# Whole 128x128 transposes in a window-attention kernel, in place of blocks cut to 64 or 96 query rows

## The chip, the cores and the metric

The kernel runs on one core of a Trainium2 chip. The metric is the time of one execution on the device, in microseconds (us), the median of several runs. The core has engines that run side by side, each through its own list of instructions in order, tied together by semaphores: TensorE (PE: matrix products and transposes, with the loads of its stationary operand shown apart as PEld), VectorE (DVE), ScalarE (ACT), GpSimd (POOL), and SyncE (SP), which issues the transfers.

## The reference, cut to what matters

Windowed attention with some global tokens, then a feed-forward network. 8 batches, 8 heads, 512 local and 32 global positions, 64 numbers a head; the network is 512 to 2048 to 512, on 4352 rows.

```python
k_all, v_all = cat([k_g, k_l]), cat([v_g, v_l])
out_g = softmax(q_g @ k_all.T / 8) @ v_all                 # 32 global queries see all 544 keys
s_ll = where(abs(i - j) <= 32, q_l @ k_l.T / 8, -1e9)      # a local query sees its window ...
s_l = cat([q_l @ k_g.T / 8, s_ll])                         # ... and the 32 global keys
out_l = softmax(s_l) @ v_all
x = heads side by side                                     # [8 * 544, 512]
h = relu(x @ w_in)
out = (s * h * h + b) @ w_out
```

The result is float32. The kernel keeps most products near that by splitting an operand into a rounded part and a rest and adding the partial products.

## The kernel before, in words

Work goes by slots: one slot is one head of one half (256 queries) of one batch, 8 x 2 x 8 = 128 slots. A half has two blocks of 128 queries. The scores of a block are a tile with the 128 queries on the partitions and 192 or 224 keys in the columns; both blocks' columns lie side by side in `sm`, 416 columns (line 30). After the softmax (lines 192 to 217) the weights must have the keys on the partitions for the product with the values, so they are transposed on PE, in two chunks of 128 key columns for a block (table `CHUNKS`, line 32). The first chunk's keys reach only a part of the block's queries, 64 or 96 of them; the second has the global keys and is wanted for all 128. A slot so has four transposes (`p_transposes`, line 287): one of 64 query rows, one of 96 and two of 128. In the first half the 64 rows are queries 64 to 127, in the second 0 to 63. They fill 64 + 128 + 96 + 128 = 416 columns of one PSUM tile `ps_t`.

From slot 16 on (`NF`), ACT copies `ps_t` to SBUF as the rounded part (`p_split`, line 361), DVE makes the rest (line 362), and the products with the values (`pv_products`, line 372) follow in the next slot, woven in between the next head's transposes by `transposes_and_pv` (line 391). Slots 0 to 15 use plain float32 products (`transposes32`, `pv32`) while the network's weights are being brought from float64 words into split float32 by DVE, ACT and POOL (`weight_piece`, line 105; 32 pieces).

The feed-forward runs behind, 12 slots later (`LAG`): each step is 24 products of 256 columns (`ffn_in`, line 494), an activation of ACT and DVE (lines 500 to 511), and 12 products of 512 columns (`ffn_out`, line 526). The global queries' weights are transposed as whole blocks (`g_transposes`, line 424), four and then one for a group of heads.

The order on each engine is set by a list scheduler when the program is built; it goes by its own estimates, and the source order is only its start. A change of one kind of instruction so moves others.

Of the kernel before, what the change touches and what calls it, by code (L numbers as in the profile page):

```python
# [18 lines left out]
B, H, SL, SG, D = 8, 8, 512, 32, 64  # L19
DM, DF = 512, 2048  # L20
P = 128
HALF = 256
KW = 224
NEG = -8.0e9
# A block's columns: [32 keys before | own 128 | 32 global | 32 keys after]; the sequence's first block has
# [32 global | own 128 | 32 keys after], its last [32 keys before | own 128 | 32 global].
# Per (half, block): the columns within the half's 416, and the two chunks of 128 of them that are  # L27
# transposed and meet the values: (first column, first query, queries). The first chunk's keys reach
# a part of the queries only, the second has the global keys.
NC = 416  # L30
COLS = {(0, 0): slice(0, 192), (0, 1): slice(192, NC), (1, 0): slice(0, 224), (1, 1): slice(224, NC)}
CHUNKS = {
# [6 lines left out]
BIG = 3.0e38  # L39


# The first batch's heads run with plain float32 products while the weights are being prepared.
NF = 16
AHEAD = 0
LAG = 12
# Where a piece of the weights is prepared: buffers that have no other use yet.
SPOTS = (["a","b","c","c","xs"]+["c","c","a","b"]*1+["a","b","c","c"]*12)[:32]
PIECES = [2, 2, 2, 2, 2, 2, 2, 2, 2, 2, 3, 3, 3, 3]
NORM_POOL = lambda j: j < NF
# [11 lines left out]
def f32(ap):  # L61
    return ap.bitcast(F32)
# [3 lines left out]
def window_attention_then_ffn(ctx: ExitStack, tc: tile.TileContext, qd, qg, kw, vw, vg, w_in, w_out, sv, bv, out):  # L66
    nc = tc.nc
# [8 lines left out]
    ident = const.tile([P, P], F32, name="ident")  # L76
# [1 line left out]
    s_t = const.tile([P, 1], F32, name="s_t")  # L78
    b_t = const.tile([P, 1], F32, name="b_t")

    # additive masks over a block's columns
    masks = {}
    for first, parts in ((True, ((32, 192, 0),)), (False, ((0, 160, 0), (192, 224, 32)))):
        mask = const.tile([P, 192 if first else 224], BF16, name=f"mask{int(first)}")
        nc.gpsimd.memset(mask, 0.0)
        # the window's key c - skip against query p: p <= c - skip <= p + 64
        for c0, c1, skip in parts:
            for sign, base in ((1, c0 - skip), (-1, 64 - c0 + skip)):
                nc.gpsimd.affine_select(
                    out=mask[:, c0:c1], in_=mask[:, c0:c1], pattern=[[sign, c1 - c0]], compare_op=ALU.is_ge,  # L90
                    fill=NEG, base=base, channel_multiplier=-sign,
                )
        masks[first] = mask
# [3 lines left out]

    xg_d = dram.tile([B * SG, DM], F32, name="xg_d")

    # The weights come as float64: a piece's words are put together as float32, with the exponent  # L100
    # bounded to float32's range (smaller is 0, larger not finite) and the mantissa rounded.
    exp_b = const.tile([P, 1], F32, name="exp_b")
    nc.vector.memset(exp_b, -896.0 * 2.0**23)

    def weight_piece(k):
        c = k // 2
        spot = SPOTS[k]
        queue = nc.scalar if k < ACT_DMA else nc.sync
        if spot == "xs":
            both = sb.tile([P, 2048], I32, tag="xs", name=f"wst{k}", bufs=1)  # L110
            st, e = both[:, 0:1024], both[:, 1024:1536]
        else:
            tags = {"a": ("kq", 1024, 3, "vsg", 1280, 1), "b": ("pg", 1280, 1, "qgs", 512, 1), "g": ("g", 1024, 2, "r", 512, 2),
                    "c": ("kq", 1024, 3, "vs", 512, 2)}
            t1, n1, b1, t2, n2, b2 = tags[spot]
            st = sb.tile([P, n1], I32, tag=t1, name=f"wst{k}", bufs=b1)[:, 0:1024]
            e = sb.tile([P, n2], I32, tag=t2, name=f"we{k}", bufs=b2)[:, 0:512]
        if k % 2 == 0:
            queue.dma_start(st, w_in[c])
            hi, lo = wi[:, 0, :, c * P:(c + 1) * P], wi[:, 1, :, c * P:(c + 1) * P]  # L120
            shape = lambda ap: ap.rearrange("p (c f) -> p c f", c=4)
        else:
            queue.dma_start(st, w_out[c * P:(c + 1) * P, :])
            hi, lo = wo[:, 0, c, :], wo[:, 1, c, :]
            shape = lambda ap: ap
        words = st.rearrange("p (n w) -> p n w", w=2)
        low, high = words[:, :, 0], words[:, :, 1]
        # 2^e with the sign
        nc.vector.tensor_scalar(  # L129
            out=e, in0=high, scalar1=20, scalar2=0x7FF, op0=ALU.logical_shift_right, op1=ALU.bitwise_and,  # L130
        )
        nc.scalar.activation(out=e, in_=e, func=AF.Relu, bias=exp_b, scale=2.0**23)
        nc.scalar.activation(out=low.bitcast(F32), in_=low.bitcast(U32), func=AF.Copy, scale=2.0**-52)
        nc.vector.scalar_tensor_tensor(  # L134
            out=e, in0=high, scalar=-(1 << 31), in1=e, op0=ALU.bitwise_and, op1=ALU.bitwise_or,
        )
        # 1 + the mantissa: 8 + 20 bits of the high word, less 7, and the low word
        nc.vector.tensor_scalar(  # L138
            out=high, in0=high, scalar1=0xFFFFF, scalar2=0x41000000, op0=ALU.bitwise_and, op1=ALU.bitwise_or,
        )  # L140
        m = high.bitcast(F32)
        nc.vector.scalar_tensor_tensor(out=m, in0=m, scalar=7.0, in1=low.bitcast(F32), op0=ALU.subtract, op1=ALU.add)  # L142
        w = f32(e)
        nc.gpsimd.tensor_tensor(out=w, in0=m, in1=w, op=ALU.mult)
        nc.scalar.copy(out=hi, in_=shape(w))
        (nc.gpsimd if k in POOL_LO else nc.vector).tensor_sub(out=lo, in0=shape(w), in1=f32(hi))

# [1 line left out]
    NS = B * 2 * H  # L149
    st_ = {}  # L150

    def slot(j):
        return j // 16, (j // 8) % 2, j % 8
# [62 lines left out]
            )  # L216
        st_["p", j] = sm

    # a half's keys for the global queries: the global ones and 0 to 223, or 224 to 511
    def own(k, hf):  # L220
        n, c = (192, P) if hf == 0 else (240, 144)
        return k[:, 0:2 * n].rearrange("p (k c) -> p k c", k=2)[:, :, 0:c]

    def sg_rows(j):
        b, hf, h = slot(j)
        if hf == 0 and h % 4 == 0:
            st_["sg", b, h // 4] = sb.tile([P, SGW], F32, tag=f"sg{h // 4}", name=f"sg{j}", bufs=1)
        r0 = 32 * (h % 4)
        return st_["sg", b, h // 4][r0:r0 + 32]
# [47 lines left out]
    def chunks(j):  # L277
        b, hf, h = slot(j)
        o = 0
        for blk in range(2):  # L280
            for c in range(2):
                c0, q0, n = CHUNKS[hf, blk][c]
                yield blk, c, c0, q0, n, slice(o, o + n)
                o += n

    # yields after each block's transposes
    def p_transposes(j):
        sm = st_.pop(("p", j))
        p_t = ps.tile([P, 512], F32, tag="t", name=f"ps_t{j}")
        st_["pst", j] = p_t[:, 0:NC]  # L290
        for blk, c, c0, q0, n, o in chunks(j):
            q = slice(q0, q0 + n)
            nc.tensor.transpose(out=p_t[:, o], in_=sm[q, c0:c0 + P], identity=ident[q, q])  # L293
            if c == 1:
                yield

# [41 lines left out]
    def scores(j):  # L338
        b, hf, h = slot(j)
        ks, qs = st_.pop(("ks", j)), st_.pop(("qs", j))  # L340
        p_s = ps.tile([P, 512], F32, tag="s", name=f"ps_s{j}")
        for blk in range(2):
            cols = COLS[hf, blk]
            for a in range(2):
                nc.tensor.matmul(  # L345
                    p_s[:, cols], lhsT=qs[:, a, blk * P:(blk + 1) * P], rhs=ks[:, cols], start=(a == 0), stop=(a == 1),
                )
        p_g = ps.tile([P, 512], F32, tag="g", name=f"ps_g{j}")
        qgh = st_["qgs", b][:, h]
        ng = 256 + 32 * hf  # L350
        nc.tensor.matmul(p_g[0:64, 0:ng], lhsT=qgh, rhs=own(ks, hf), start=True, stop=True)  # L351
        softmax(j, p_s)
        # rows of the global queries: qh.k + ql.k
        tg = sb.tile([P, 288], F32, tag="tg", name=f"tg{j}", bufs=1)
        nc.scalar.copy(out=tg[0:32, 0:ng], in_=p_g[32:64, 0:ng])
        nc.vector.tensor_add(out=sg_rows(j)[:, hf * 256:hf * 256 + ng], in0=p_g[0:32, 0:ng], in1=tg[0:32, 0:ng])
# [7 lines left out]

    xcur = {}

    # yields after each block's products
    def pv_products(j):
        pt, vs = st_.pop(("pt", j)), st_.pop(("vs", j))
        p_o = st_["pso", j] = ps.tile([P, 2, 2, P], F32, tag="o", name=f"ps_o{j}")  # L370
# [16 lines left out]
            out=x[q0:q0 + 64, h // 2, :].rearrange("p (k q) -> p k q", k=2), in0=u[0:64], in1=u[64:128],  # L387
        )

    # The last products of a block are shorter than the load of the next values' chunk: transposes go between.  # L390
    def transposes_and_pv(jt, jp):
        t = p_transposes(jt) if NF <= jt < NS else iter(())
        p = pv_products(jp) if NF <= jp < NS else iter(())
# [6 lines left out]
        if NF <= jt < NS:  # L400
            p_split(jt)

# [1 line left out]
    def g_softmax(b, g):  # L404
        v = st_["sg", b, g]
        gm = sb.tile([P, 1], F32, tag="gm", name=f"gm{b}_{g}")
# [20 lines left out]
            nc.scalar.copy(out=ph, in_=v)  # L427
            nc.vector.tensor_sub(out=pl, in0=v, in1=f32(ph))

    # by pairs of heads  # L430
    def g_load(b, h):
        rv = sb.tile([P, 10 * D], F32, tag="rvg", name=f"rvg{b}_{h}", bufs=1)
        nc.sync.dma_start(rv, vg[b, h // 2])
# [20 lines left out]
        nc.vector.tensor_add(out=xr.rearrange("q (h d) -> q h d", h=2), in0=t[:, :, 0], in1=t[:, :, 1])  # L454
        nc.sync.dma_start(xg_d[b * SG:(b + 1) * SG, h * D:(h + 2) * D], xr)

# [1 line left out]
    NT = 17  # L458
    xs_ = {}

# [114 lines left out]
    piece = 0  # L575
# [3 lines left out]
    for j in range(NM + LAG + 2):  # L579
# [3 lines left out]
        for _ in range(PIECES[j] if j < len(PIECES) else 0):  # L583
            weight_piece(piece)
            piece += 1
# [106 lines left out]
```

## Time and profile before

| what | value |
|---|---|
| median of 3 runs | 1111.67 us (1111.55 to 1111.82) |
| profiled execution, first to last instruction | 1109.8 us |
| PE busy | 1064.7 us, 96% |
| DVE busy | 872.3 us, 79% |
| ACT busy | 722.4 us, 65% |
| POOL busy | 426.9 us, 38% |
| granted TensorE clock, mean share of full speed | 0.984 |

The median is 1.9 us over the profiled span; the profile gives no other time for its own execution than this span. A matmul's end in the trace is modelled and matmuls overlap, so a row's busy time is not what the matmul costs; the distance from one start to the next, or the length of a piece in the chain of waits, is.

### The profile page before, as it was taken

Reading aid. Unit: us, or ns where it says so; the run is one execution under the profiler, and the core shown is the slowest. Engines: PE = TensorE matmul, PEld = TensorE weight load, DVE = VectorE, ACT = ScalarE, POOL = GpSimd, SP = SyncE. Lnnn points to the kernel's source line nnn. Section 1 sums busy time; section 2 is a strip of 40 time slices with the busy share of each in tenths; the row PEclk is TensorE's granted clock in tenths of the full one; section 3 lists DMA queues with packets and bytes.
Section 4 is the critical chain, followed back from the end, with each engine's and each line's share of the span. In section 5 each row is a group of like instructions: output and inputs, shape, how many; then the busy total and the mean of one; then the engine's idle time right before and its main releaser. Section 6 shows DMA issues by size and latency. Waiting matters only on the chain.

```text
span 1109.8 us, 20489 instructions
## 1 busy us (share of the span) xinstructions
PE 1064.7 (96%) x7048; PEld 930.7 (84%) x7048; DVE 872.3 (79%) x2119; ACT 722.4 (65%) x1828; POOL 426.9 (38%) x457
## 2 busy tenths in 40 slices
PE   4889879999999999999999999999999999999996
PEld 2457668889989889898998999989989899998885
DVE  7999998789778977798778977897789777964221
ACT  6666767677667766686767775776678676844221
POOL 6887774343224423343323433442344242411000
PEclk9968999999999999999999999999999999999998
DMA  6454422232213212231223221321223121201000
GB/s 231 149 164 140 153 67 87 69 95 72 63 50 93 77 37 93 66 91 54 82 62 95 67 69 46 106 72 44 78 65 100 45 93 56 85 6 45 20 20 19
DMA packets 63536, 86.80 MB, mean 78 GB/s; under 512 B 7624, under 2 KB 50632, under 8 KB 63432
## 3 DMA queue, kind: packets, MB, share of 16 engines
q1 hardware_dynamic: 63144, 84.44, 24.9%
q8 instruction: 56, 0.92, 0.3%
q10 hardware_dynamic: 288, 1.05, 0.2%
q14 instruction: 48, 0.39, 0.1%
HBM read 76.02 MB, written 9.44 MB: 77 GB/s over the span
## 4 chain that ended last, share of the span: by engine, by line
PE 84%; DVE 12%; issue 1%; DMA 1%; ACT 0%; POOL 0%; DVEq 0%
PE acc L526 33%; PE ps_h L494 32%; PE ps_t L293 7%; PE ps_s L345 4%; PE ps_o L372 4%; DVE we L134 2%; DVE wst L138 2%; DVE we L129 2%; PE ps_og L446 2%; DVE wst L142 2%; PE ps_g L351 1%; DVE g L509 1%; DVE ss L210 1%; DVE sm L201 1%; PE ps_tg L424 1%
## 5 line engine op out<-in xcount | busy, mean ns | idle before, releaser
L494 PE MATMUL ps_h<-xs,wi 128*128 128x256 f32 x3264 | 445.4, 283 | 3.1 <-DVE r L501 2.0
L526 PE MATMUL acc<-wo,g 128*128 128x512 f32 x1632 | 431.1, 399 | 4.9 <-DVE g L509 2.7
L494 PEld LDWEIGHTS ps_h<-xs,wi 128*128 128x128 f32 x3264 | 420.2, 190 | 18.2 <-DVE r L501 2.5
L526 PEld LDWEIGHTS acc<-wo,g 128*128 128x128 f32 x1632 | 289.9, 189 | 59.5 <-DVE g L509 3.6
L189 POOL TENSOR_TENSOR vs<-rv,vs 128x256 fp32r<-128x256 f32 x112 | 94.9, 847 | 221.4 <-ACT vs L188 215.6
L501 DVE SCALAR_TENSOR_TENSOR r<-ps_h,s_t,r 128x512 f32<-128x512 f32 x136 | 101.5, 746 | 70.6 <-ACT r L500 70.1
L508 ACT ACTIVATE g<-r,b_t 128x512 fp32r<-128x512 f32 x136 | 98.2, 722 | 63.4 <-DVE r L501 62.5
L509 DVE SCALAR_TENSOR_TENSOR g<-r,b_t,g 128x512 fp32r<-128x512 f32 x136 | 109.3, 803 | 38.2 <-ACT g L508 36.5
L500 ACT ACTIVATE r<-ps_h 128x512 f32<-128x512 f32 x136 | 81.1, 597 | 85.8 <-PE ps_h L494 77.7
L181 POOL TENSOR_TENSOR kq<-rq,kq 128x256 fp32r<-128x256 f32 x112 | 90.1, 805 | 116.0 <-ACT kq L180 108.6
L207 ACT ACTIVATE sm<-sm,nm 128x224 f32<-128x224 f32 (+1 forms) x256 | 118.5, 467 | 18.1 <-DVE nm L201 17.0
L293 PE MATMUL ps_t<-ident,sm 128*128 128x128 f32 (+2 forms) x512 | 115.5, 291 | 1.4 <-ACT x L316 0.8
L179 POOL TENSOR_TENSOR kq<-rk,kq 64x416 fp32r<-64x416 f32 x56 | 62.0, 1108 | 120.9 <-ACT kq L178 112.5
L201 DVE CUSTOM_DVE_ANT_0 sm<-ps_s,mask 128x224 f32<-128x224 f32 (+1 forms) x256 | 85.2, 366 | 20.3 <-PE ps_t L293 10.8
L293 PEld LDWEIGHTS ps_t<-ident,sm 128*128 128x128 f32 (+2 forms) x512 | 64.9, 143 | 32.1 <-issue 6.1
L438 POOL TENSOR_TENSOR vsg<-rvg,vsg 128x320 fp32r<-128x320 f32 x64 | 58.8, 938 | 84.4 <-ACT vsg L437 84.3
L214 DVE TENSOR_SCALAR sm<-sm,ss 128x192 f32<-128x192 f32 (+1 forms) x224 | 86.8, 430 | 3.4
L372 PE MATMUL ps_o<-pt,vs 128*128 128x256 f32 x448 | 84.5, 284 | 0.0
L345 PE MATMUL ps_s<-kq 128*128 128x192 f32 (+1 forms) x448 | 77.7, 279 | 2.8 <-DVE kq L179 1.2
L345 PEld LDWEIGHTS ps_s<-kq 128*128 128x128 f32 x448 | 67.6, 194 | 9.3 <-DVE kq L179 1.5
L372 PEld LDWEIGHTS ps_o<-pt,vs 128*128 128x128 f32 x448 | 69.8, 195 | 3.1
L361 ACT CAST pt<-ps_t 128x416 fp32r<-128x416 f32 x112 | 57.0, 509 | 15.2 <-PE ps_t L293 14.7
(82 smaller groups left out, 1389.8 us busy)
## 6 DMA issues: line engine op xcount, KB each, us to landing
rq<-in_qd SPq DMA_DIRECT2D x128, 128.0 KB, 2.2
rv<-in_vw SPq DMA_DIRECT2D x128, 128.0 KB, 2.1
rk<-in_kw SPq DMA_DIRECT2D x64, 208.0 KB, 2.4
rvg<-in_vg SPq DMA_DIRECT2D x32, 320.0 KB, 2.9
out<-o SPq DMA_DIRECT2D x34, 256.0 KB, 3.0
wst<-in_w_in SPq DMA_DIRECT2D x15, 512.0 KB, 3.8
wst<-in_w_out SPq DMA_DIRECT2D x15, 512.0 KB, 3.8
rqg<-in_qg SPq DMA_DIRECT2D x8, 128.0 KB, 2.8
```

Of the source, the lines that this page charges most:

```text
L181: nc.gpsimd.tensor_sub(out=qs[:, 1, :], in0=rq, in1=f32(qs[:, 0, :]))
L189: nc.gpsimd.tensor_sub(out=vs[:, :, 1, :], in0=rv4, in1=f32(vs[:, :, 0, :]))
L201: nc.vector.tensor_tensor_reduce(out=sm[:, c], in0=p_s[:, c], in1=mask, op0=ALU.add, op1=ALU.min, scale=-scale, scalar=BIG, accum_out=nm[: ...
L207: nc.scalar.activation(out=p, in_=p, func=AF.Exp, bias=nm[:, blk:blk + 1], scale=-1.0, accum_out=ss[:, blk:blk + 1],)
L293: nc.tensor.transpose(out=p_t[:, o], in_=sm[q, c0:c0 + P], identity=ident[q, q])
L345: nc.tensor.matmul(p_s[:, cols], lhsT=qs[:, a, blk * P:(blk + 1) * P], rhs=ks[:, cols], start=(a == 0), stop=(a == 1),)
L372: nc.tensor.matmul(p_o[:, blk, :, q0:q0 + n], lhsT=vs[:, 2 * blk + c], rhs=pt[:, :, o], start=(c == 1), stop=(c == 0),)
L494: nc.tensor.matmul(p_h[:, k], lhsT=wi[:, a, c, f * P:(f + 1) * P], rhs=xs[:, e, c, :], start=(n == 0), stop=(n == 11),)
L501: nc.vector.scalar_tensor_tensor(out=r, in0=p_h, scalar=s_t, in1=r, op0=ALU.mult, op1=ALU.mult)
L508: nc.scalar.activation(out=g[:, 0], in_=r, func=AF.Identity, bias=b_t)
L509: nc.vector.scalar_tensor_tensor(out=g[:, 1], in0=r, scalar=b_t, in1=f32(g[:, 0]), op0=ALU.add, op1=ALU.subtract,)
L526: nc.tensor.matmul(oacc[t][i], lhsT=g[:, a, k, i * P:(i + 1) * P], rhs=wo[:, e, f, :], start=(pr == 0 and n == 0), stop=(pr == 7 and n == 5),)
```

## The change

`p_transposes` transposes all 128 query rows of every chunk. The 64 or 32 columns that come out beyond the wanted ones are placed so that a later transpose of the same head overwrites them, or so that they lie outside the 416 columns that `p_split` reads. In the first half of the queries `ps_t` is read from column 64 on. What is read, and where the later products find it, stays the same. The other hunks only blank out comments; because of three added lines, a line number from 297 up is 3 higher in the changed kernel.

```diff
     def p_transposes(j):
         sm = st_.pop(("p", j))
         p_t = ps.tile([P, 512], F32, tag="t", name=f"ps_t{j}")
-        st_["pst", j] = p_t[:, 0:NC]
+        first = 64 if slot(j)[1] == 0 else 0
+        st_["pst", j] = p_t[:, first:first + NC]
         for blk, c, c0, q0, n, o in chunks(j):
-            q = slice(q0, q0 + n)
-            nc.tensor.transpose(out=p_t[:, o], in_=sm[q, c0:c0 + P], identity=ident[q, q])
+            at = first + o.start - q0
+            nc.tensor.transpose(out=p_t[:, at:at + P], in_=sm[:, c0:c0 + P], identity=ident)
             if c == 1:
                 yield
```

In the first half the four transposes go to columns 0, 128, 256 and 352, and the last overwrites 32 columns of the third. In the second half they go to 0, 96, 224 and 288, and the second and the fourth overwrite 32 and 64 columns of the one before.

PE, in the middle of the program, a head whose transposes stand in pairs between the products with the values (`ps_o`) of the head before; `ps_s` are scores and `ps_h` is the feed-forward. Before:

```order
L345 MATMUL ps_s_7128<-kq_7017 128x192
L372 MATMUL ps_o_7078<-pt_6982,vs_6985 128x256
L372 MATMUL ps_o_7078<-pt_6982,vs_6985 128x2x64
L293 MATMUL ps_t_7081<-ident,sm_6923 128x64
L293 MATMUL ps_t_7081<-ident,sm_6923 128x128
L372 MATMUL ps_o_7078<-pt_6982,vs_6985 128x256
L372 MATMUL ps_o_7078<-pt_6982,vs_6985 128x2x96
L293 MATMUL ps_t_7081<-ident,sm_6923 128x96
L293 MATMUL ps_t_7081<-ident,sm_6923 128x128
L345 MATMUL ps_s_7128<-kq_7017 128x192
L494 MATMUL ps_h_7354<-xs_6635,wi 128x256 x13
```

The same head in the changed kernel:

```order
L497 MATMUL ps_h_7259<-xs_6635,wi 128x256 x7
L348 MATMUL ps_s_7128<-kq_7017 128x224 x2
L375 MATMUL ps_o_7078<-pt_6982,vs_6985 128x256
L375 MATMUL ps_o_7078<-pt_6982,vs_6985 128x2x64
L296 MATMUL ps_t_7081<-ident,sm_6923 128x128 x2
L375 MATMUL ps_o_7078<-pt_6982,vs_6985 128x256
L375 MATMUL ps_o_7078<-pt_6982,vs_6985 128x2x96
L296 MATMUL ps_t_7081<-ident,sm_6923 128x128 x2
L348 MATMUL ps_s_7128<-kq_7017 128x192 x2
L497 MATMUL ps_h_7259<-xs_6635,wi 128x256 x16
```

The pairs stand where they stood, each now of two whole blocks; the feed-forward step beside them is one step earlier in the chain (`ps_h_7259`, not `ps_h_7354`), so attention stands about a slot further ahead of it than before.

PE, the head before that one, whose four transposes stand in a row between feed-forward products. Before:

```order
L494 MATMUL ps_h_7259<-xs_6635,wi 128x256
L293 MATMUL ps_t_6971<-ident,sm_6807 128x64
L293 MATMUL ps_t_6971<-ident,sm_6807 128x128
L293 MATMUL ps_t_6971<-ident,sm_6807 128x96
L293 MATMUL ps_t_6971<-ident,sm_6807 128x128
L494 MATMUL ps_h_7259<-xs_6635,wi 128x256 x4
```

And in the changed kernel:

```order
L497 MATMUL ps_h_7149<-xs_6635,wi 128x256 x11
L354 MATMUL ps_g_6805<-kq_6689,qgs_6172 64x256
L296 MATMUL ps_t_6971<-ident,sm_6807 128x128 x4
L497 MATMUL ps_h_7149<-xs_6635,wi 128x256 x13
L529 MATMUL acc_0_6887<-wo,g_7075 128x512 x6
```

Again only the shape of the transposes and the feed-forward step around them differ.

DVE, at the end of the opening, around the last step of the last piece of the weights (`wst`, line 142); `nm` belongs to the softmax, and `r`, `g` to the feed-forward. Before:

```order
L501 SCALAR_TENSOR_TENSOR r_1495<-ps_h_1470,s_t,r_1495 128x512
L146 TENSOR_TENSOR wo<-we_937,wo 128x512
L201 ISA sm_1241,nm_1242<-ps_s_1234,mask_73 128x192
L201 ISA nm_1242 128x1
L201 ISA sm_1241,nm_1242<-ps_s_1234,mask_81 128x224
L201 ISA nm_1242 128x1
L142 SCALAR_TENSOR_TENSOR wst_960<-wst_960 128x512
```

And in the changed kernel:

```order
L512 SCALAR_TENSOR_TENSOR g_1498<-r_1495,b_t,g_1498 128x512
L201 ISA sm_1241,nm_1242<-ps_s_1234,mask_73 128x192
L201 ISA nm_1242 128x1
L201 ISA sm_1241,nm_1242<-ps_s_1234,mask_81 128x224
L201 ISA nm_1242 128x1
L142 SCALAR_TENSOR_TENSOR wst_936<-wst_936 128x512
```

The same head's softmax stands before the last piece in both, with the last two pieces in the other order; this instruction is number 267 of DVE's list in both kernels.

## Rows read from the trace of the kernel before

**Rows 1.** The page's busy times: us, share of the span, instructions.

```profile
PE 1064.7 (96%) x7048; PEld 930.7 (84%) x7048; DVE 872.3 (79%) x2119; ACT 722.4 (65%) x1828; POOL 426.9 (38%) x457
```

**Rows 2.** The page's chain that ended last, shares of the span by engine.

```profile
PE 84%; DVE 12%; issue 1%; DMA 1%; ACT 0%; POOL 0%; DVEq 0%
```

**Rows 3.** Busy times by stretch; the first line names the columns.

```profile
core 0: us, PE busy (x) PEld busy (x) DVE busy (x) ACT busy (x) POOL busy (x), PEclk, DMA share, GB/s
0.00:165.00 165.00, 131.25 (x584) 89.96 (x584) 155.40 (x279) 108.75 (x243) 125.86 (x114) 0.92 0.48 152
165.00:1000.00 835.00, 834.05 (x5816) 752.29 (x5817) 682.71 (x1791) 581.97 (x1530) 295.76 (x337) 1.00 0.23 70
1000.00:1109.00 109.00, 99.40 (x650) 88.43 (x648) 34.17 (x51) 31.67 (x57) 5.28 (x6) 0.97 0.08 27
...
404.00:523.50 119.50, 119.50 (x835) 107.84 (x835) 98.12 (x259) 83.92 (x222) 43.33 (x49) 1.00 0.24 72
```

**Rows 4.** All waits of PE, 165 to 1000 us: us, times, longest.

```profile
PE ps_t L293 <- DVE pg L428: 0.6, 1, 0.6
PE ps_h L494 <- DVE xs L467: 0.2, 1, 0.2
```

**Rows 5.** Waits of PE's weight loads, same stretch.

```profile
PEld acc L526 <- DVE g L509: 0.3, 1, 0.3
```

**Rows 6.** The chain in order of time, 511 to 519: start, us, what.

```profile
512.21 0.44 PE ps_tg L424 x4
512.64 0.41 PE ps_o L372 x4
513.05 2.27 PE ps_h L494 x19
515.32 2.33 PE acc L526 x10
517.65 0.66 PE ps_t L293 x4
518.31 0.47 PE acc L526 x2
```

**Rows 7.** The chain, 536 to 541, a head with its pairs apart.

```profile
537.25 0.19 PE ps_o L372 x2
537.44 0.47 PE ps_t L293 x2
537.90 0.21 PE ps_o L372 x2
538.12 0.20 PE ps_t L293 x2
```

**Rows 8.** PE's instructions near 512 and 517, singly: start, us (end modelled).

```profile
512.04 0.27 PE L424 MATMUL ps_tg<-ident,sg 128*128 128x128 f32 x1
512.15 0.49 PE L424 MATMUL ps_tg<-ident,sg 128*128 128x128 f32 x3
...
517.49 0.25 PE L293 MATMUL ps_t<-ident,sm 96*128 96x96 f32 x1
517.58 0.27 PE L293 MATMUL ps_t<-ident,sm 128*128 128x128 f32 x1
517.78 0.53 PE L293 MATMUL ps_t<-ident,sm 64*128 64x64 f32 x2
518.07 0.48 PE L526 MATMUL acc<-wo,g 128*128 128x512 f32 x1
```

**Rows 9.** Groups of PE in 165 to 1000: count, busy us, mean ns.

```profile
L293 PE MATMUL ps_t<-ident,sm 128*128 128x128 f32 x224 | 65.9, 301 | 0.0
L293 PE MATMUL ps_t<-ident,sm 64*128 64x64 f32 x112 | 30.5, 272 | 0.6 <-DVE pg L428 0.6
L293 PE MATMUL ps_t<-ident,sm 96*128 96x96 f32 x112 | 27.9, 249 | 0.0
```

## Prediction, made before the changed kernel ran

> **What bounds the kernel now.** I first read the busy shares and the chain that ended last: PE is busy 96% of the span and makes up 84% of the chain, DVE 12% [rows 1, 2]. A share over the whole span can hide stages, so the next view is busy time by stretch [rows 3]. There are three. In the opening, up to 165 us, DVE is busy 155.4 of 165 us and PE only 131: the weights are prepared, and DVE sets the pace. From 165 to 1000 us PE is busy 834 of 835 us and DVE 683. After 1000 us only feed-forward is left, again on PE (99 of 109). Inside the middle stretch one batch of 16 slots takes 119.5 us, PE without a gap, DVE 98.1 us of it, ACT 83.9 [rows 3].
>
> "PE busy" alone could still be PE waiting inside overlapped matmuls, so the waits come next: in 835 us PE waits twice, for 0.8 us together [rows 4], and its weight loads wait once for the feed-forward's DVE step, for 0.3 us [rows 5]. Nothing else is late. What PE's instructions cost one after the other is therefore what the middle stretch costs, and a saving there shortens the span one for one until something else is late.
>
> **What the transposes cost now.** Ends of matmuls are modelled, so the mean durations of rows 9 say little: there the 64-row block costs nearly what a 96-row one does. The chain in order of time is the view to use, since each piece in it runs from the end of the one before to its own end and the pieces add up to the span.
>
> A head whose four transposes stand in a row takes 0.66 us for them [rows 6]. A head with its pairs apart takes 0.47 us for the pair that has the 64-row block and 0.20 us for the pair with the 96-row block [rows 7], together 0.67. So the two pairs differ by 0.27 us although the slow one is the smaller. The starts show where that sits: 96 rows to the next start 0.09 us, the 128-row block to the 64-row block 0.20, the 64-row block and the last one 0.29 together to the next product [rows 8]. Time goes where a 64-row transpose is entered and where it is left, not in its columns.
>
> The Trainium skill has a rule for this: in "TensorEngine Tiling (Array Packing)", section "Tiling Modes", under its key properties, it says that changing the tiling mode drains TensorE, and lists 64 rows, not 96, as a mode. The trace agrees, 0.20 us on either side of a 64-row block and 0.09 behind a 96-row one; the drain itself is in no row.
>
> **What takes their place.** The trace of before has whole-block transposes of the same kind: the global queries' (same tile `ident`, 128 rows, 128 columns, four in a row). Four of them take 0.44 us in the chain [rows 6], and the step from the first to the second is 0.11 us [rows 8]. That is the price I take for the new transposes, whether in fours or in pairs: a pair costs 0.22, close to the 0.20 of the 96-row pair [rows 7], which meets no change of mode.
>
> **The sum.**
> - Removed: 0.66 us a head, by the head in a row (0.67 by the head in pairs).
> - Added: 0.44 us a head.
> - Saved: 0.22 us a head. The middle stretch has 112 blocks of each part shape [rows 9], so 112 heads: 112 x 0.22 = 24.6 us.
> - Heads of the opening: 16, at the same 0.22 at most 3.5 us. DVE is the bound there [rows 3], so PE's saving becomes idle time: counted 0, with 3.5 as the lower end.
> - ACT's copy and DVE's rest read 416 columns as before, from column 64 on in half of the heads: no instruction more or longer. Counted 0; no row shows a shift of that kind with another duration.
> - A transpose now reads all 128 partitions of `sm`. The softmax writes all of them in the same instructions as before, so it is ready no later. Counted 0.
> - The scheduler's new order. In the middle PE does the same products in another weave; since it waits 0.8 us in 835, order can hardly win there. In the opening it can win or lose: the last weight step is DVE's instruction 267 in both kernels, with the same softmaxes and seven feed-forward steps ahead of it, so weights should be ready at about the same time. DVE has 165 - 155.4 = 9.6 us of idle time in the opening, which bounds what a better order wins; a worse one could cost about one slot, 119.5 / 16 = 7.5 us. Taken as 0, by the place that stays the same; I keep -3 to +6 for this and the waits below, on top of the sum.
> - More of the feed-forward is left for the end: 687 of its products stand behind the last transpose, before 622. They only move from one PE-bound stretch to another.
>
> The profiled span is 1109.8 us, and 1109.8 - 24.6 = 1085.2; the runs' median lies 1.9 us above the span, and I carry that over: 1111.67 - 24.6 = 1087.0 us.
>
> What is late next? A batch becomes 119.5 - 16 x 0.22 = 116.0 us, of which DVE needs 98.1, or 85% instead of 82%, and ACT 83.9, or 72%. Neither becomes the bound, and 112 heads save the full amount unless single waits grow.
>
> **Rivals.**
> 1. *Waits come up behind PE.* The feed-forward's weight loads wait for DVE's step `g` once now, 0.3 us [rows 5]. With PE 3% faster and a new order, such a wait could come in each slot. For it: the new order puts the feed-forward about a slot later against attention, so PE may stand at a step whose `g` is younger. Against: DVE and ACT keep 15% and more of a batch free, and almost nothing waits now. At 0.1 us in each of 112 slots it costs 11.2 us: 1098 us.
> 2. *Columns are what costs.* A head's transposes grow from 64 + 128 + 96 + 128 = 416 to 512 columns. The feed-forward's 24 products of 256 columns and 12 of 512 are priced by columns in the trace (10 of 512 in 2.33 us [rows 6], so 0.455 ns a column), and if only that counted, 96 columns more would cost 0.044 us a head, 4.9 us over 112 heads: 1116.6 us. Against: 0.66 us for 416 columns and 0.44 us for 512 in one stretch of 7 us [rows 6]. [...]
> 3. *Overwriting makes the second transpose wait* (the slower side). Where a transpose writes columns that the one before has just written, PE might have to finish the first. That is one pair a head in first halves and two in second halves, 56 x 1 + 56 x 2 = 168 pairs. A single whole transpose lasts 0.27 us by its row, its successor starts after 0.11 [rows 8]: 0.16 us a pair, 26.9 us in all, more than the 24.6 won: 1114.0 us. It decides from 0.15 us a pair. No row of before has overlapping writes. Against: both are PE's own instructions, which finish in order, and the order shows no added wait between them.
>
> **How the numbers follow.** Forecast 0.87, rival 1 0.08, rival 2 0.02, rival 3 0.03. The likeliest gives 1087.0. Its range goes from 1087.0 - 3.5 = 1083.5, with a little of a better opening, so 1083, to 1087.0 + 6 = 1093; that leaves out most of the rivals and the ends of the order's effect, some 2 in 10. A difference of 0.2%, about 2.2 us, is what a measurement of this kernel can tell from no change. Forecast and rival 1 are faster by more; rival 3 sits at that edge and rival 2 beyond it: faster 0.95, within 0.2% 0.02, slower 0.03.
>
> **What would show it.** In the profile after, four transposes in a row should take about 0.44 us in the chain and a pair 0.22, and the batches should repeat every 116 us; the opening should end near 165 us. Rival 1 would show as more than a few us of PE waits between 165 and 1000, rival 3 as pairs of 0.38 us in second halves against 0.22 in the pair of a first half that doesn't overlap, rival 2 as a pair that costs more than 0.47. The prediction is wrong if the fours take 0.44 and the span still falls by less than 18 us, or if it falls by more than 29.

## The result, and the profile after

The changed kernel takes 1097.41 us (median of 4 runs, 1096.15 to 1100.02) against 1111.61 us before: a ratio of 0.9876, 95% interval 0.9862 to 0.9890. That is 14.2 us faster, where 24.6 us were forecast; 1097.4 lies outside the range of 1083 to 1093. The four runs lie 3.9 us apart, so a difference from this kernel holds to a microsecond or two and not to a tenth. The profiled execution has a span of 1095.0 us, 14.8 less than before.

The page's busy times and its chain, as in [rows 1, 2]:

```profile
PE 1042.3 (95%) x7048; PEld 927.3 (85%) x7048; DVE 856.1 (78%) x2119; ACT 723.5 (66%) x1828; POOL 416.1 (38%) x457
...
PE 82%; DVE 11%; issue 2%; ACT 1%; DMA 1%; POOL 1%; SPq 0%; DVEq 0%; POOLq 0%; ACTq 0%
```

PE is still the bound, but ACT and POOL now have 1% each of the chain, where they had 0%, and "issue" (time in which an engine waited for nothing that the profile shows) has 2%, where it had 1%. The price of the transposes, from the chain in order of time, as in [rows 6]: start, us, what.

```profile
503.93 0.44 PE ps_tg L427 x4
...
509.16 0.44 PE ps_t L296 x4
```

A head's four transposes in a row now take what the global queries' take, 0.44 us instead of 0.66. So the price of a row of four came out as forecast. The busy times by stretch, as in [rows 3]: the middle, one late batch (from a head's first transpose to the same one 16 slots on) in the kernel before and in the changed kernel, and a piece of 20 us in both, again the kernel before first:

```profile
165.00:1000.00 835.00, 830.25 (x5937) 763.85 (x5936) 683.07 (x1814) 594.36 (x1556) 293.38 (x344) 1.00 0.25 73
...
766.40:885.93 119.53, 119.53 (x836) 107.89 (x835) 98.51 (x258) 84.08 (x221) 43.35 (x49) 1.00 0.24 72
747.50:863.79 116.29, 116.29 (x837) 107.28 (x836) 96.84 (x258) 84.48 (x221) 41.87 (x49) 1.00 0.25 74
...
225.00:245.00 20.00, 20.00 (x147) 18.21 (x146) 16.40 (x43) 15.26 (x40) 8.74 (x10) 1.00 0.33 96
225.00:245.00 20.00, 16.18 (x110) 14.57 (x110) 15.83 (x44) 12.79 (x38) 8.64 (x10) 0.91 0.31 90
```

A late batch takes 116.3 us, close to the 116.0 that were forecast. But between 225 and 245 us PE does 110 matmuls, where the kernel before does 147, and stands still for 3.8 us. All of PE's waits in 165 to 1000 us, as in [rows 4]:

```profile
PE ps_h L497 <- DVE xs L470: 2.6, 1, 2.6
PE ps_g L354 <- DVE sg L359: 0.7, 1, 0.7
PE ps_s L348 <- POOL kq L179: 0.5, 1, 0.5
PE ps_s L348 <- POOL kq L181: 0.4, 1, 0.4
PE ps_o L375 <- DVE pt L365: 0.3, 1, 0.3
```

They were 0.8 us and are 4.5 us, and four of the five lines belong to the place near 230 us. The chain there shows what PE waited for:

```profile
226.27 2.81 PE acc L529 x12
...
229.39 0.15 PE ps_g L354
...
232.05 0.91 ACT sm L207 x4
...
233.93 1.83 DVE sm L214 x2
235.76 0.73 DVE xr L457
...
237.08 0.62 DVE xs L470
...
237.74 4.27 PE ps_h L497 x21
```

From 229.5 to 237.7 us the span runs through ACT and DVE, not through PE, which does the attention of two heads there and waits in between. Then comes a second cost, the clock. After the wait of 2.6 us that ends at 237.7, the granted clock falls to half, the lower of its two levels (1.2 GHz in place of 2.4), from 238.4 to 241.8 us. The stretch, and 21 products of the feed-forward elsewhere in this kernel, to set beside the last line above:

```profile
238.40:241.80 3.40, 3.40 (x18) 3.40 (x17) 2.47 (x8) 0.51 (x2) 0.00 (x0) 0.50 0.66 203
...
504.78 2.52 PE ps_h L497 x21
```

The 21 products behind the stall take 4.27 us where 2.52 is usual, 1.75 us more. The order on PE, which was set before the run, has this at that place (number, line, what; `ps_t_2268` and `ps_t_2363` are two heads, `ps_h` and `acc` the feed-forward):

```
337 L296 MATMUL ps_t_2268<-ident,sm_2110 128x128
...
344 L348 MATMUL ps_s_2308<-kq_2204 128x192 x2
345 L449 MATMUL ps_og_6_2175<-vsg_6_2075,pg_1_1796 64x128 x10
346 L348 MATMUL ps_s_2402<-kq_2297 128x224 x2
347 L348 MATMUL ps_s_2402<-kq_2297 128x192 x2
348 L375 MATMUL ps_o_2360<-pt_2279,vs_2282 128x256
349 L375 MATMUL ps_o_2360<-pt_2279,vs_2282 128x2x96
350 L296 MATMUL ps_t_2363<-ident,sm_2220 128x128 x2
```

Between these two heads stands no feed-forward product. Every other two successive heads of the middle stretch have 14 or more between them, in both kernels. The products that stand between the two heads' transposes wait, for 1.2 us together, for splits that POOL and DVE make (`kq`, `pt`). The longest wait, 2.6 us, is of the feed-forward's product that stands behind both heads: its input `xs` comes from DVE behind softmax steps (`sm`), as the chain shows. PE goes by its list and has no feed-forward product to do meanwhile.

### The profile page after: what moved, and what is told of

Same layout as the page of the kernel before. It is cut to its first block, busy times and chain, and to the rows that moved or that the text cites. A ratio compares the mean times of both kernels' runs of the same rounds, so it can differ in the third digit from the quotient of the medians.

```text
span 1095.0 us, 20539 instructions
## 1 busy us (share of the span) xinstructions
PE 1042.3 (95%) x7048; PEld 927.3 (85%) x7048; DVE 856.1 (78%) x2119; ACT 723.5 (66%) x1828; POOL 416.1 (38%) x457
## 4 chain that ended last, share of the span: by engine, by line
PE 82%; DVE 11%; issue 2%; ACT 1%; DMA 1%; POOL 1%; SPq 0%; DVEq 0%; POOLq 0%; ACTq 0%
PE ps_h L497 32%; PE acc L529 32%; PE ps_t L296 5%; PE ps_s L348 4%; PE ps_o L375 4%; PE ps_og L449 2%; DVE we L134 2%; DVE wst L142 1%; DVE wst L138 1%; PE ps_g L354 1%; DVE we L129 1%; DMA rk<-in_kw 1%; DVE sm L201 1%; PE ps_s L267 1%; DVE ss L210 1%
## 5 line engine op out<-in xcount | busy, mean ns | idle before, releaser
L497 PEld LDWEIGHTS ps_h<-xs,wi 128*128 128x128 f32 x3264 | 415.7, 190 | 17.2 <-DVE xs L470 3.1
L529 PEld LDWEIGHTS acc<-wo,g 128*128 128x128 f32 x1632 | 293.2, 190 | 62.8 <-ACT g L511 2.9
L189 POOL TENSOR_TENSOR vs<-rv,vs 128x256 fp32r<-128x256 f32 x112 | 86.8, 775 | 188.0 <-ACT vs L188 185.3
L296 PE MATMUL ps_t<-ident,sm 128*128 128x128 f32 x512 | 102.0, 289 | 2.1 <-POOL sm L214 2.1
L348 PE MATMUL ps_s<-kq 128*128 128x192 f32 (+1 forms) x448 | 74.0, 276 | 2.8 <-POOL kq L179 2.4
L214 DVE TENSOR_SCALAR sm<-sm,ss 128x192 f32<-128x192 f32 (+1 forms) x224 | 73.9, 372 | 3.2
L348 PEld LDWEIGHTS ps_s<-kq 128*128 128x128 f32 x448 | 65.4, 190 | 8.6 <-POOL kq L179 3.0
L389 DVE TENSOR_TENSOR x<-u 64x256 f32<-64x256 f32 x112 | 68.9, 615 | 3.6
L375 PEld LDWEIGHTS ps_o<-pt,vs 128*128 128x128 f32 x448 | 67.5, 190 | 2.8 <-DVE pt L365 0.5
L296 PEld LDWEIGHTS ps_t<-ident,sm 128*128 128x128 f32 x512 | 59.0, 145 | 12.0 <-issue 5.3
```

Of the source, the lines that this page charges most:

```text
L189: nc.gpsimd.tensor_sub(out=vs[:, :, 1, :], in0=rv4, in1=f32(vs[:, :, 0, :]))
L296: nc.tensor.transpose(out=p_t[:, at:at + P], in_=sm[:, c0:c0 + P], identity=ident)
L348: nc.tensor.matmul(p_s[:, cols], lhsT=qs[:, a, blk * P:(blk + 1) * P], rhs=ks[:, cols], start=(a == 0), stop=(a == 1),)
L375: nc.tensor.matmul(p_o[:, blk, :, q0:q0 + n], lhsT=vs[:, 2 * blk + c], rhs=pt[:, :, o], start=(c == 1), stop=(c == 0),)
L497: nc.tensor.matmul(p_h[:, k], lhsT=wi[:, a, c, f * P:(f + 1) * P], rhs=xs[:, e, c, :], start=(n == 0), stop=(n == 11),)
L529: nc.tensor.matmul(oacc[t][i], lhsT=g[:, a, k, i * P:(i + 1) * P], rhs=wo[:, e, f, :], start=(pr == 0 and n == 0), stop=(pr == 7 and n == 5),)
```

## Experiments

The scheduler's order and the shape of the blocks came together in the change. To part them, the first experiments alter the shape of the transposes in the finished program, after the scheduler has set the order, so that every engine's list is that of one kernel while the blocks are those of the other. The kernel before is timed beside each.

**Whole blocks, order of before.** The source emits the cut blocks (at the columns that the change uses), and the program is then walked through:

```diff
+def whole_blocks(nc, wanted):          # after scheduling, before the launch
+    ...
+                q0, c0 = divmod(sm.offset, NC)
+                rep = lambda a, off: a.__replace__(ap=((a.ap[0][0], P), (1, P)), offset=off)
+                blk.instructions[k] = i.__replace__(
+                    ins=(rep(idn, 0), rep(sm, c0)), outs=(rep(out, out.offset - q0),),
+                    tile_size=(P, P), tile_position=(0, 0),
+                )
+    whole_blocks(nc, lambda rows: rows < P)
```

> Whole blocks as in the change, but every engine's list in the order of the kernel before (the transposes are widened after scheduling). Theory 1, the price of the blocks was right and the scheduler's new order ate the rest: 112 x 0.22 us come in full, about 1087 us, within 2 us, with no wait of PE over 1 us between 170 and 1000 us. Rival, the blocks themselves save less than the rows of before say: no better than the changed kernel, about 1097 us.

Measured: 1092.0 us (1091.55 to 1092.28), ratio 0.9823 (0.9809 to 0.9838). Neither number came: 5.4 us better than the changed kernel, so the order did cost something, and 5 us short of the forecast gain (1087). Two things make up the 5. The chain of a second-half head, in which both pairs overwrite, and of a first-half head, to set beside [rows 7]:

```profile
497.23 0.22 PE ps_t L295 x2
497.45 0.18 PE ps_o L374 x2
497.64 0.23 PE ps_t L295 x2
...
528.98 0.19 PE ps_o L374 x2
529.17 0.24 PE ps_t L295 x2
529.41 0.21 PE ps_o L374 x2
529.62 0.22 PE ps_t L295 x2
```

One pair of a head costs 0.22, the other 0.23 or 0.24: it is the one behind the short product of 128 columns. The saving is 0.67 - 0.46 = 0.21 for a first-half head. Over all 112 heads the intervals around the transposes, compared matmul by matmul with the kernel before (same order, so they pair off), sum up to 23.2 us less, which is 1.4 below the forecast. Between the transposes PE loses 3.6 us, by the same comparison. PE's waits and its weight loads' waits from 170 us on name the place (before, weight loads waited 0.2 us on `sg`, and PE for no other engine at all; that wait on `sg` is one of four lines that stand beside the one shown in [rows 5]):

```profile
PE ps_g L353 <- DVE sg L358: 1.2, 3, 0.6
PE acc L528 <- DVE g L511: 0.6, 1, 0.6
...
PEld acc L528 <- DVE g L511: 2.6, 6, 1.0
PEld ps_g L353 <- DVE sg L358: 2.2, 5, 0.8
```

The two places come back in most batches, where the global queries' softmax is on DVE. One of them in the chain, where `sg` in line 415 is the softmax's last multiply:

```profile
252.17 1.31 DVE sg L415
...
256.13 0.66 DVE r L503
...
256.82 0.46 DVE sg L358
...
257.33 0.35 PE ps_g L353
```

The changed kernel itself has little of this: behind 245 us its PE waits once for another engine, 0.7 us for `sg`, and its weight loads 1.0 us in all; here it is 1.8 and 4.8 us.

**Cut blocks, order of the changed kernel.** The reverse: the changed source, and after scheduling the blocks are cut back to 64 and 96 rows.

```diff
+                blk.instructions[k] = i.__replace__(
+                    ins=(rep(idn, q0 * P + q0, n, n), rep(sm, q0 * NC + sm.offset, n, P)),
+                    outs=(rep(out, out.offset + q0, P, n),),
+                    tile_size=(64 if n == 64 else P, P), tile_position=(q0, 0),
+                )
```

> The blocks cut to 64 and 96 rows as before, but every engine's list in the order of the changed kernel. Theory 1: what the order costs shows alone, 1111.6 plus about 8 to 10, that is 1120 to 1122 us. Rival, the order costs nothing: 1111.6 us.

Measured: 1121.5 us (1120.81 to 1121.86), ratio 1.0087 (1.0070 to 1.0104). The new order alone costs 9.8 us, and whole blocks in it bring 24.1 us, nearly the 24.6 of the forecast. Its piece from 225 to 245 us and its longest wait there:

```profile
225.00:245.00 20.00, 16.35 (x99) 14.32 (x98) 16.51 (x45) 12.15 (x36) 8.10 (x9) 0.86 0.32 92
...
PE ps_h L497 <- DVE xs L470: 2.4, 1, 2.4
```

It is the changed kernel's stall, with the old blocks. It belongs to the order. The granted clock falls behind it here too, to 0.86 in the mean of the 20 us against 0.91 in the changed kernel, so a part of the 24.1 lies there and not in the transposes.

The opening is later as well. DVE's last step of the weights (`wst`) starts at 158.0 us in the kernel before, at 160.4 in the changed kernel and at 162.1 here; the lines of the first two:

```profile
L142 DVE SCALAR_TENSOR_TENSOR wst<-wst x32: 672/692/1780, 9.6 to 158.0; 128x512 f32<-128x512 f32 x32
L142 DVE SCALAR_TENSOR_TENSOR wst<-wst x32: 676/688/1798, 8.7 to 160.4; 128x512 f32<-128x512 f32 x32
```

**The changed kernel without that place.** A small edit elsewhere makes the scheduler choose again, and it no longer puts those two heads next to each other:

```diff
-        nc.vector.tensor_scalar_mul(v, v, gs)
+        nc.vector.tensor_scalar_mul(v[:, 0:272], v[:, 0:272], gs)
+        nc.vector.tensor_scalar_mul(v[:, 272:SGW], v[:, 272:SGW], gs)
```

> The changed kernel, with one edit that moves the order: the global softmax's last multiply on DVE in two halves of 272 columns. The scheduler then no longer puts two heads' transposes one after the other with no feed-forward product between (it did so once, near 230 us). Theory: that place alone cost 6.6 us, so 1097.4 - 6.6 = about 1091 us, and no wait of PE over 1 us between 170 and 1000. Rival, the order costs in many places: 1096 us or more.

Measured: 1092.18 us (1091.92 to 1092.36), ratio 0.9829 (0.9816 to 0.9843), 5.2 us below the changed kernel. The piece from 225 to 245 us:

```profile
225.00:245.00 20.00, 20.00 (x152) 18.65 (x151) 17.39 (x44) 15.67 (x41) 8.97 (x10) 1.00 0.36 101
```

PE works through, at the full clock. The edit also splits a DVE instruction and sets a new order everywhere, so the 5.2 us are not that place alone. An estimate from the traces parts them: count every product of PE at the mean distance from start to start that its shape has between 285 and 1000 us, and put what the starts lie further apart down to the stretch. Between 225 and 245 us the changed kernel then loses 6.8 us more than this run, and 6.8 more than whole blocks in the old order. Before 225 us it loses 1.9 less than this run and 1.1 more than whole blocks in the old order; behind 245 us as much as this run, within 0.2, and 2.3 less than whole blocks in the old order. So the place costs about what the expectation says, and this run gives some of it back in a longer opening.

**The remaining waits.** Whole blocks, order of before, and the global softmax's last multiply shortened:

```diff
+                cut = lambda a: a.__replace__(ap=(a.ap[0], (1, 64)))      # of (1, 544)
+                blk.instructions[k] = i.__replace__(
+                    ins=(cut(i.ins[0]),) + tuple(i.ins[1:]), outs=(cut(o),) + tuple(i.outs[1:]))
```

> Whole blocks in the order of the kernel before; the global softmax's last multiply works on 64 of its 544 columns, the rest of the global weights stays without its division. Theory: the 3.6 us that PE lost there at two places a batch come from DVE, which is late behind that 1.3 us multiply, so about 1092.0 - 3 = 1089 us. Rival, PE waits there for ACT or for itself: 1092 us.

Measured: 1089.49 us (1088.27 to 1089.91), ratio 0.9803 (0.9790 to 0.9817): 2.5 us below the same kernel with the full multiply. The matmul-by-matmul comparison has 1.7 us left of the 3.6 between the transposes. The multiply itself in the full and in the short form, and the waits left in the short one:

```profile
L415 DVE TENSOR_SCALAR sg<-sg,gs 128x544 f32<-128x544 f32 x14 | 14.9, 1065 | 0.2
```

```profile
L415 DVE TENSOR_SCALAR sg<-sg,gs 128x64 f32<-128x64 f32 x14 | 11.3, 807 | 0.2
```

```profile
PE ps_g L353 <- DVE sg L358: 0.8, 2, 0.7
...
PEld ps_g L353 <- DVE sg L358: 1.4, 3, 0.9
```

From 170 us on, the feed-forward's wait for `g` is gone, and the one for `sg` is a third smaller. So PE waits there for DVE, which is late behind the global softmax; a multiply that is on the average only 0.26 us shorter is enough to halve it.

**Which part of a cut block costs.** Only the 64-row blocks whole, by `wanted` = 64 rows, order of before:

```diff
-    whole_blocks(nc, lambda rows: rows < P)
+    whole_blocks(nc, lambda rows: rows == 64)
```

> Only the 64-row blocks are made whole, the 96-row blocks stay cut; order of the kernel before. Theory, entering and leaving the 64-row form is the whole cost: a head takes 0.22 + 0.20 = 0.42 us instead of 0.66, 112 x 0.24 = 26.9, about 1084.7 us, some 2 us below whole blocks in the same order. Rival, any cut block costs: half of what whole blocks bring, about 1099 us.

Measured: 1089.84 us (1089.12 to 1090.33), ratio 0.9804 (0.9789 to 0.9819). It is 2.2 us better than all blocks whole, as expected, and as far above its forecast as that one was. Leaving out the 96-row blocks costs nothing; their 32 columns more are the 2.2 us.

Then the 64-row blocks that start at row 0 keep their rows and columns, and only the tile size in the instruction changes:

```diff
+                if type(i).__name__ == "InstMatmult" and i.is_transpose and tuple(i.tile_size) == (64, P):
+                    if tuple(i.tile_position) == (0, 0):
+                        blk.instructions[k] = i.__replace__(tile_size=(P, P))
```

> The 64-row blocks of the second halves (rows 0 to 63) keep their 64 rows and columns, and only the tile size that their instruction names goes from 64x128 to 128x128, as the 96-row blocks have it; order of the kernel before. Theory, the change of tiling mode is the cost: 56 pairs fall from 0.47 to about 0.19 us, 15 us less, about 1096 us. Rival, it is the 64 rows or the start and not the mode: no change, 1111.6 us.

Measured: 1101.74 us (1100.78 to 1102.56), ratio 0.9911 (0.9896 to 0.9926), 9.9 us faster, where 15 were expected. The chain of a second-half head, first the pair with 96 rows, last the one with 64, and of a first-half head, whose 64-row block comes first and was left as it was:

```profile
502.11 0.20 PE ps_t L293 x2
502.31 0.18 PE ps_o L372 x2
502.49 0.19 PE ps_t L293 x2
...
534.14 0.47 PE ps_t L293 x2
534.60 0.21 PE ps_o L372 x2
534.82 0.20 PE ps_t L293 x2
```

The same second-half head in the kernel before has 0.46 for that last pair:

```profile
505.22 0.46 PE ps_t L293 x2
```

The pair with 64 rows costs 0.19 in the wider mode and 0.46 or 0.47 in its own, as it did in [rows 7]. The price fell in full, 56 x 0.27 = 15 us. What is missing are waits again:

```profile
PE ps_g L351 <- DVE sg L356: 3.2, 6, 1.0
PE acc L526 <- DVE g L509: 0.6, 1, 0.6
```

**A version that is better than both.** Order of before; 64-row blocks whole in first halves, 64 rows with the 128-row tile size in second halves, 96-row blocks left. It is the kernel with only the 64-row blocks whole, and:

```diff
+                if q0 == 0:
+                    blk.instructions[k] = i.__replace__(tile_size=(P, P))
+                    continue
```

> Order of the kernel before; 64-row blocks whole in first halves, and in second halves 64 rows with the tile size 128x128; 96-row blocks stay. Theory: against only the 64-row blocks whole (1089.8 us), 56 pairs fall from 0.22 to 0.195 us, 1.5 us, so about 1088.3. Rival, PE now waits for the other engines and gives it all back: 1089.8.

Measured: 1088.52 us (1087.72 to 1089.27), ratio 0.9795 (0.9781 to 0.9808). It came out as forecast, but its interval overlaps that of only the 64-row blocks whole, so the 1.3 us between them are not shown. With the multiply in two halves, and a new order with it:

> As the one with mixed 64-row blocks, and the multiply in two halves, so that the scheduler makes a new order (no two heads in a row in it). Theory: DVE can put a step that PE waits for between the halves; 1085 to 1088 us. Rival, two instructions cost DVE more and the new order brings waits elsewhere: 1089 us or more.

Measured: 1087.73 us (1086.93 to 1088.81), ratio 0.9790 (0.9777 to 0.9803), the fastest here, 9.7 us below the changed kernel. Against the mixed kernel the intervals overlap; PE waits 2.2 us in 165 to 1000 us, none for `sg`.

## Why the prediction was wrong

The prediction named a sign of its own being wrong, and it came: the fours take 0.44 us, and the span falls by 14.8 us, less than 18.

- *What bounds the kernel:* right. PE sets the time in the middle, and still does outside the 20 us near 230. One reading was too quick: [rows 5] shows one line of the five that this view has, so "nothing else is late" was not quite so. Another of the five is 0.2 us on `sg`, where PE itself waits once the blocks are whole and the order is the old one.
- *What the old transposes cost and why:* right. Entering and leaving the 64-row tiling mode was the cost; the tile size alone, with the same rows and columns, takes a pair from 0.46 to 0.19 us.
- *The new price:* 0.44 us for four in a row, as forecast; 0.46 for two pairs, forecast 0.44. A late batch of the changed kernel takes 3.2 us less than before, forecast 3.5, which over 112 heads leaves some 2 of the missing 10 us; matmul by matmul, in the old order, it is 1.4.
- *Opening counted 0:* not quite. The last step of the weights kept its place in DVE's list, but starts 2.4 us later, and by the estimate above the changed kernel loses 1.1 us more before 225 us than whole blocks in the old order do. In the old order, where by the same matmul-by-matmul comparison the first 165 us of PE's list change by 0.1 us, the 0 was right.
- *"Order can hardly win there", counted 0:* **this step failed.** I saw that PE had no waits to lose and concluded that order hardly mattered, with -3 to +6 for all of it. That it can bring waits I allowed for only in the opening, by a place that stayed the same. The new order costs 9.8 us over the whole program with the cut blocks and 5.4 us with the whole ones. About 7 us arise at one place near 230 us in the middle, two heads with no feed-forward product between: PE stands still for 3.8 us, then runs 21 products at the lower clock for 1.75 us more than usual; the rest of the 7 is not parted. The prediction had no term for the clock.
- *"Neither becomes the bound, and 112 heads save the full amount unless single waits grow":* the condition decided, but not in the same place in both orders. DVE's share of a batch was as computed. In the old order DVE is late at the global softmax, behind several instructions in a row, and PE, 3% faster, arrives before it: 3.6 us. In the changed kernel these waits are nearly absent, and the stall near 230 us stands in their stead.
- *Rival 1* gave a time of 1098 us, near the measured one, for waits behind PE. That is luck: its place was wrong (a wait in every slot for `g`; it was one long stall, with the clock behind it), and so was the 0.08.
- *Rivals 2 and 3:* out. Four blocks of 128 columns are cheaper than 416 columns, and a second-half head, in which both pairs overwrite, costs what a first-half head does, in which one does.

The miss in measured pieces, in the order that the changed kernel has: whole blocks bring 24.1 us, the order takes 9.8, which leaves 14.3; measured 14.2. In the old order whole blocks bring only 19.7, and the order then takes 5.4. Both ways add up because each is a difference of the same times. That they split differently says that the two prices hang on each other: what waits behind DVE take from the blocks in the old order, they hardly take in the new one.

## What to carry to other kernels

A saving on the engine that is the bound comes in full only as far as the others' work is ready earlier too: look for the places, once a batch or so, where several of their instructions stand in a row, and price the arrival of the faster engine there. Where a scheduler makes the order anew, read its lists for stretches in which the bound engine has only work that depends on the others, as the two heads here without a feed-forward product between; it was to be seen before the run. A stall can cost more than the time that the engine stands still, if its clock falls behind it. To part a shape's price from a new order, change the shape in the finished program and keep the lists; do it in both orders, since the price found in one need not hold in the other.

## What the runs showed of the hardware

- A transpose of 64 rows named with a 64x128 tile costs its pair 0.46 us; the same with a 128x128 tile 0.19 us. "TensorEngine Tiling (Array Packing)" of the Trainium skill, section "Tiling Modes", says that a change of mode drains; these runs agree, for rows, as far as the 0.27 us go, and the drain itself is in no row. For a product with 64 output columns among 128-column ones no such step shows: the chain's piece for `ps_g` (128*64, 288 columns) is 0.12 us, in the order of before with whole blocks (`527.85 0.12 PE ps_g L353`).
- After a stall in which PE stood still for 3.8 us of 20, the granted clock fell from 2.4 to 1.2 GHz for 3.4 us, and 21 products took 4.27 us instead of 2.52.
- A DVE multiply of 64 columns instead of 544 took 0.81 us instead of 1.07 on the average, far from an eighth.
